# First channel product of the last two groups as seven products of quarters, interleaved with the second

## The chip, the cores and the metric

One core of a Trainium2 chip. The metric is the device time of one execution in microseconds; lower is better. Engines: PE (matmul), DVE, ACT and POOL (elementwise), SP (issues DMAs).

## The reference

Eight batches of linear attention (8 heads, 576 tokens, 64 wide), then an MLP mixer over tokens and over channels. What the change touches is the last step, the channel MLP, on `u` of shape (8, 576, 512):

```
u  = x + (relu(x^T @ w_tok1) @ w_tok2)^T        # 576 -> 256 -> 576 along the tokens
h2 = relu(u @ w_ch1) @ w_ch2                    # 512 -> 1536 -> 512 along the channels
out = u + h2
```

Inputs and output are f32; the kernel multiplies in bf16 and accumulates in f32.

## The kernel before, in words

**Groups.** A batch has 576 tokens: four tiles of 128 and a half tile. `group(g)` for g = 0 to 7 is the four full tiles of batch g (512 tokens); group 8 (`B`) holds the half tiles of all eight batches, again 512 rows. Each group goes through two products: the first, `mlp1` (L315), turns the transposed rows `uT` (channels on the partitions) and `wc1` (512 x 1536) into `h1T` (1536 channels x 512 rows): 12 chunks of 128 channels, each four matmuls of 512 columns, evicted with a relu by ACT (one of the twelve by DVE, L331 and L333). The second is already done by seven products in place of eight: `mlp2_unit` (L372) multiplies quarters of `h1T` and of `wc2`, or sums of quarters, into four PSUM banks called A, X, F and E. A unit is a half of one of the seven products: 6 matmuls of 256 columns (L386); fourteen units make the product. `s_sums` (L356) makes the sums of `h1T` quarters (S1 to S4, bf16) on DVE, `mlp2_sums` (L397) makes the four quarters of the result out of the banks: one copy by ACT (L407), adds out of PSUM by DVE (L409 to L438), and adds of the residual `u` by POOL (L404, six of 128x256 for each group). The results lie in `res`; `store` (L448) writes them out by two DMAs on POOL's queue for each half, `store_tails` (L458) those of group 8 on SP and ACT.

**Order.** The program is scheduled by hand (`manual_schedule`): each engine runs its instructions in the order in which the code issues them, and waits come from the data. For groups 1 to 8 a loop (L1008) runs 26 slots: 12 chunks of the first product in the order `order`, then 14 units of the second. `plan_of(g)` (L933) hangs the other work of the batch pipeline (loads, features, attention, token MLP, transposes) on the slots. Groups 7 and 8 have no such work left but `s_sums`: batch 7, the last, is finished in the slots of group 6 (token MLP at slots 8 to 13, `uT` transposes by DMA from slots 15 and 16, L272; the half tile at slot 18, L298, L303, L306, L307).

**PSUM.** Two tiles `psA` of two banks, four `psM` of one bank; `nextM` and `nextA` hand them out in turn.

**Buffers.** The inputs of the batches are loaded into `raw["q"]`, `raw["k"]`, `raw["v"]` (two buffers each), features in `kp`, `qp`, their transposes in `qpT`. Once the last batch has passed, these are free.

Of the kernel before, what the change touches and what calls it, by code (L numbers as in the profile page):

```python
# [9 lines left out]
F32 = mybir.dt.float32  # L10
BF16 = mybir.dt.bfloat16
I32 = mybir.dt.int32
AF = mybir.ActivationFunctionType
# [5 lines left out]
def kernel(  # L19
# [11 lines left out]
    nc = tc.nc  # L31

    B, H, S, D = q.shape
    F = 2 * D
    Dm = H * D
    D_tok = moe_w_tok1.shape[1]
    D_ch = moe_w_ch1.shape[1]
    P = 128
    assert S == 9 * (P // 2) and D == 64 and H == 8 and B % 2 == 0
    NCC = Dm // P  # L40
    NT = D_tok // P
    NCH = D_ch // P
# [22 lines left out]
    wc1 = sb("w_ch1", [P, NCC, D_ch], BF16)  # L65
    wc2 = sb("w_ch2", [P, NCH, Dm], BF16)

    raw = {n: [sb(f"{n}_raw{i}", [P, H, NJ, D], F32) for i in range(2)] for n in "qkv"}
    kp = [sb(f"kp{j}", [P, H, 2, D], BF16) for j in range(NJ)]
    qp = [sb(f"qp{j}", [P, H, 2, D], BF16) for j in range(NJ)]  # L70
    vb = [sb(f"vb{j}", [P, H, VP], BF16) for j in range(NJ)]

    qpT = sb("qpT", [P, H, NJ, P], BF16)
    at_T = (0, 1, 3, 4, 2)
    kv_sb = sb("kv_sb", [P, H, VP], BF16)
    x_sb = sb("x_sb", [P, T, Dm], BF16)
# [4 lines left out]
    u_sb = [sb(f"u_sb{i}", [P, T, Dm], F32) for i in range(2)]  # L81
# [5 lines left out]
    h1T = sb("h1T", [P, NCH, 4 * P], BF16)  # L87
# [14 lines left out]
    def rows_of(t, i):  # L102
        b = t.rearrange("p h n d -> p h (n d)").bitcast(BF16)
        return b[:, 0:NQ, i * DQ:(i + 1) * DQ]
# [4 lines left out]
    T3, T4 = B12, k1_of[2]  # L109
    S_of = {1: (rows_of(raw["k"][0], 0), rows_of(raw["k"][0], 1), k1_of[0], S4_sb)}  # L110
    for g in range(2, B + 1):
        S_of[g] = (k1_of[0], k1_of[1], rows_of(raw["v"][1], 0), S4_sb)

    LO, HI = slice(0, P // 2), slice(P // 2, P)
    psM, psA = [], []
# [2 lines left out]
    def nextM():  # L118
        cnt["M"] += 1
        return psM[(cnt["M"] - 1) % 4]  # L120

    def nextA():
        cnt["A"] += 1
        return psA[cnt["A"] % 2]
# [185 lines left out]
    def group(g):  # L310
        if g < B:
            return uT[g % 2], u_sb[g % 2]
        return uTt, u_tl
# [42 lines left out]
    def s_sums(g, c0, c1):  # L356
        V = nc.vector
        s1, s2, s3, s4 = [x[:, c0:c1, :] for x in S_of[g]]
        a11, a21 = h1T[:, c0:c1, 0:2 * P], h1T[:, c0:c1, 2 * P:4 * P]
        a12, a22 = h1T[:, NQ + c0:NQ + c1, 0:2 * P], h1T[:, NQ + c0:NQ + c1, 2 * P:4 * P]  # L360
        V.tensor_add(s1, a21, a22)  # L361
        V.tensor_sub(s2, s1, a11)
        if g > 1:
            V.tensor_sub(s3, a11, a21)
        V.tensor_sub(s4, a12, s2)
# [6 lines left out]
    def mlp2_unit(g, i):  # L372

        pr, tt = divmod(i, 2)
        S1, S2, S3, S4 = S_of[g]
        a, w, bank = ((h1T[:, 0:NQ, 0:2 * P], B11, "A"), (S2, T2, "X"), (S3, T3, "F"), (S1, T1, "E"),
                      (h1T[:, NQ:NCH, 0:2 * P], B21, "A"), (h1T[:, NQ:NCH, 2 * P:4 * P], T4, "F"),
                      (S4, B22, "E"))[pr]
        if pr < 4 and tt == 0:
            mbank[bank] = [nextM()[:, 0:2 * DQ].rearrange("p (t d) -> p t d", t=2)] * 2  # L380
            if bank == "E" and g == B:
                mbank["E"][1] = nextA()[:, 0, :].rearrange("p (t d) -> p t d", t=2)
        m = mbank[bank]
        own = m[0] is not m[1]
        for c in range(NQ):
            nc.tensor.matmul(m[tt][:, tt, :], a[:, c, tt * P:(tt + 1) * P], w[:, c, :],  # L386
                             start=(pr < 4 and c == 0 and (tt == 0 or own)),
                             stop=(c == NQ - 1 and (tt == 1 or own) and (pr > 3 or bank == "X")),
                             skip_group_check=True)

    def quarter(g, i, k):

        cols = slice(k * DQ, (k + 1) * DQ)
        return res_all[:, i, :, cols], group(g)[1][:, 2 * i:2 * i + 2, cols]

    def mlp2_sums(g, i):
        V, G = nc.vector, nc.gpsimd  # L397
# [45 lines left out]
    def flush():  # L443
        while stores:
            stores.pop(0)()

    def store(g, t, r):
        if g < B:  # L448
            if t % 2 == 1:
                o = out[g].rearrange("(i n) d -> i n d", n=9)  # L450
                j = t - 1
                nc.gpsimd.dma_start(out=o[:, j:j + 2, :], in_=r[0:P:2, :, :])
                nc.gpsimd.dma_start(out=o[:, 5 + j:5 + j + 2, :], in_=r[1:P:2, :, :])


    tails = out.rearrange("(t b) (i n) d -> (b i) t n d", b=2, n=9)[:, :, 4, :]

    def store_tails(t0, t1, k, eng):  # L458
        cols = slice(k * DQ, (k + 1) * DQ)
        eng.dma_start(out=tails[:, t0:t1, cols], in_=res[t0 // 2][:, t0 % 2:t0 % 2 + t1 - t0, cols])  # L460

# [303 lines left out]
    for mi in (2, 3):  # L767
        mlp1_out(mi, bank_h[mi], (A, V)[mi - 2])
    head.__exit__(None, None, None)
    psum = ctx.enter_context(tc.tile_pool(name="psum", bufs=1, space=bass.MemoryType.PSUM, reuse_waits="tile"))  # L770
    psA += [psum.tile([P, 2, 512], F32, name=f"psA{i}") for i in range(2)]
    psM += [psum.tile([P, 512], F32, name=f"psM{i}") for i in range(4)]

# [159 lines left out]
    def plan_of(g):  # L933
        b, f = g + 1, g + 2
        plan = [[] for _ in range(26)]

        def put(s, fn, *args):
            plan[s].append(lambda: fn(*args))

        if g == 1:  # L940
            put(5, tail_step, 1)
            for j in range(NJ):
                put(j // 2 + 1, f1k, b, j, 0, V)
                put((j + 1) // 2 + 2, kv_step, b, j)
                put(5 + j, num_step, b, j)
            put(3, u_out, 1, 1)
            for i, at in enumerate((4, 4, 17)):
                put(at, t_sum, (1, 3, 2)[i])
            for j in range(NJ):
                put((5, 6, 7, 8, 9)[j], f1k, f, j, 1, A)  # L950
            for j in range(2):
                put(10, f1k, f, j, 0, A)
            put(10, b1_step, b, 0)
            for j in range(2, 4):
                put(11, f1k, f, j, 0, A)
            put(11, b1_step, b, 1)
            put(11, f1k, f, 4, 0, A)
            for n in range(2):
                put(13 + n, u_step, b, n)
                put(15 + n, uturn_step, b, n)  # L960
            put(10, s_sums, g, 0, 3)
            put(11, s_sums, g, 3, 5)
            put(12, s3_sum, g)
            for j in range(3):
                put((12, 13, 15)[j], qfeat, f, j, A, A)
                put((12, 13, 17)[j], qturn_dma, f, j)
            put(17, lambda: feat(A, qp[3][:, :, 1, :], rawt("q", f)[:, :, 3, :], sin_t, 3))
            for j in range(NJ):
                put((18, 18, 19, 20, 21)[j], vcast, f, j, (A, A, V, A, A)[j])
                if j == 2:  # L970
                    put(19, lambda: feat(V, qp[3][:, :, 0, :], rawt("q", f)[:, :, 3, :], cos_t, 3))
                    put(19, qturn_dma, f, 3)
                if j == 3:
                    put(20, qfeat, f, 4, V, A)
                    put(20, qturn_dma, f, 4)
            for j in range(NJ):
                put((23, 24, 25, 25, 25)[j], kv_step, f, j)
            put(8, q_load, 4)
            put(9, v_load, 4)
            put(20, k_load, 4)  # L980
            return plan
        if b < B:
            for j in range(NJ):
                put(((2, 3, 4, 6, 7) if g == 2 else (2, 3, 4, 5, 6))[j], num_step, b, j)
            for n in range(2):
                put(8 + n, b1_step, b, n)
                put(12 + n, u_step, b, n)
                put(15 + n, uturn_step, b, n)
            put(18, tail_step, b)
        if g == 2:  # L990
            put(14, tail_turn, 1)
        for at, cs in ((7, (0, 2)), (9, (2, 4)), (11, (4, 5))):
            put(at, s_sums, g, *cs)
        if f < B:
            for j in range(NJ):
                put((7, 8, 10, 12, 13)[j], qfeat, f, j, V, A)
                put((7, 8, 10, 17, 17)[j], qturn_dma, f, j)
                put((12, 13, 14, 15, 17)[j], f1k, f, j, 0, V)
                put(13 + j, f1k, f, j, 1, A)
                put(j, vcast, f, j, G)  # L1000
                put((20, 21, 22, 24, 25)[j], kv_step, f, j)
        if f + 1 < B:
            put(0, q_load, f + 1)
            put(6, v_load, f + 1)
            put(18, k_load, f + 1)
        return plan

    for g in range(1, B + 1):  # L1008
        plan = plan_of(g)
        for s in range(len(plan)):  # L1010
            if s < NCH:
                ps = mlp1(g, order[s])
            else:
                mlp2_unit(g, s - NCH)
                mlp2_sums(g, s - NCH)
            for fn in plan[s]:
                fn()
            flush()
            if s < NCH:
                mlp1_out(order[s], ps, V if s == 10 else A)  # L1020
                if s == NCH - 1:
                    s_sums(g, NQ - 1, NQ)

    flush()
    _ = tile, bass_utils
# [30 lines left out]
```

## Time and profile before

| what | value |
|---|---|
| median of 12 runs | 262.42 us (260.57 to 264.37) |
| the profiled execution | 264.17 us |
| its span, first to last instruction | 262.4 us |
| PE busy | 250.6 us, 96% of the span |
| DVE / ACT / POOL busy | 189.7 (72%) / 155.4 (59%) / 100.9 (38%) us |
| granted PE clock, mean | 0.992 |
| first product of group 7, of group 8 | 219.45 to 229.81, 238.97 to 249.34 us |
| second product of group 7, of group 8 | 229.81 to 238.97, 249.34 to 258.52 us |

Times inside the span are counted from the first instruction. A row of the profile gives line, engine, operation, what it writes <- what it reads, the shape, the count, and then busy time and mean duration, idle time of the engine before it and who ended it. The chain of waits follows the work that ended last backwards. "PEclk" is the granted clock of PE as a share of the full one.

### The profile page before, as it was taken

The numbers are of one execution on the slowest core, as the hardware profiler recorded it, in microseconds if no ns is written. First come the engines' busy times: TensorE is split into PE (matmuls) and PEld (weight loads), VectorE is DVE, ScalarE is ACT, GpSimd is POOL, SyncE is SP. The second block draws the span as 40 slices with busy tenths as digits, with TensorE's granted clock in tenths as the row PEclk, the third lists the DMA queues.
The fourth block names the chain that finished last, engine by engine and source line by source line (L and its number), as shares of the span: only waits on it lengthen the run. The fifth ranks groups of instructions, "written<-read, shape, count | busy, mean of one in ns | idle before, by whom it ended". The sixth has DMA issues, their size and how long they took to land.

```text
span 262.4 us, 5679 instructions
## 1 busy us (share of the span) xinstructions
PE 250.6 (96%) x2098; PEld 158.2 (60%) x2110; DVE 189.7 (72%) x452; ACT 155.4 (59%) x259; POOL 100.9 (38%) x176
## 2 busy tenths in 40 slices
PE   7799999999999699999999999999999999999994
PEld 2565456455578255775587557755875576486483
DVE  5892857899989079958994899489938773563563
ACT  4763685886998267946783679367935452613610
POOL 5197457270008801194019502830291045045041
PEclk9999999999999799999999999999999999999999
DMA  6999999999999999999978996994391034003004
GB/s 207 366 374 389 390 389 380 303 259 243 262 356 219 257 217 359 210 214 318 350 154 161 373 307 145 173 307 93 68 212 71 4 80 158 24 0 146 17 0 161
DMA packets 79947, 57.18 MB, mean 218 GB/s; under 512 B 48176, under 2 KB 74928, under 8 KB 79920
## 3 DMA queue, kind: packets, MB, share of 16 engines
q1 hardware_dynamic: 76128, 47.26, 68.4%
q0 software_dynamic: 2560, 8.39, 9.4%
q10 hardware_dynamic: 1232, 1.18, 1.4%
q8 instruction: 16, 0.26, 0.4%
q14 instruction: 11, 0.09, 0.1%
HBM read 35.85 MB, written 9.44 MB: 173 GB/s over the span
## 4 chain that ended last, share of the span: by engine, by line
PE 70%; ACT 3%; DVE 1%; DMA 1%; issue 1%; ACTq 0%
PE psM L319 31%; PE psM L386 24%; PE psA L239 5%; PE psA L257 3%; PE psA L214 3%; PE psA L190 2%; DMA uT<-u_bf 1%; PE psA L298 1%; ACT qp L145 1%; ACT u_bf L267 1%; ACT vb L161 1%; PE psA L386 1%; DVE u_sb L262 0%; DVE k_raw L368 0%; ACT kp L145 0%
## 5 line engine op out<-in xcount | busy, mean ns | idle before, releaser
L319 PE MATMUL psM<-uT,w_ch 128*128 128x512 bf16 x368 | 89.7, 384 | 2.4 <-DMA uT<-u_bf 2.4
L331 ACT ACTIVATE h1T<-psM 128x512 bf16<-128x512 f32 x93 | 55.5, 597 | 43.2 <-PE psM L319 41.5
L404 POOL TENSOR_TENSOR res<-res,u_sb 128x256 f32<-128x256 f32 x42 | 32.2, 798 | 96.2 <-DVE res L409 95.8
L319 PEld LDWEIGHTS <-w_ch 128*128 128x128 bf16 x416 | 38.4, 98 | 43.5 <-DMA uT<-u_bf 2.5
L386 PEld LDWEIGHTS <-h1T 128*128 128x128 bf16 x288 | 27.3, 98 | 5.8
L145 ACT ACTIVATE kp<-k_raw,sin_t 128x512 bf16<-128x512 f32 (+1 forms) x45 | 28.4, 669 | 1.2 <-DMA k_raw<-in_k_dram 1.2
L145 ACT ACTIVATE qp<-q_raw,sin_t 128x512 bf16<-128x512 f32 (+1 forms) x40 | 26.6, 681 | 0.1
L386 PE MATMUL psM<-w_ch,h1T 128*128 128x256 bf16 x192 | 25.0, 273 | 0.0
L163 POOL CAST vb<-v_raw 128x512 bf16<-128x512 f32 (+1 forms) x38 | 20.5, 585 | 11.4 <-DMA v_raw<-in_v_dram 10.6
L386 PE MATMUL psM<-w_ch_t,k_raw 128*128 128x256 bf16 x186 | 23.6, 273 | 0.0
L386 PEld LDWEIGHTS <-k_raw 128*128 128x128 bf16 x204 | 19.7, 98 | 5.0 <-issue 1.2
L214 PEld LDWEIGHTS <-qpT 128*128 128x128 bf16 x320 | 14.9, 98 | 9.7 <-issue 1.6
L230 DVE TENSOR_TENSOR x_sb<-psA,rden 128x512 bf16<-128x512 f32 x28 | 19.4, 691 | 1.0
L361 DVE TENSOR_TENSOR k_raw<-h1T 128x512 bf16<-128x512 bf16 (+2 forms) x31 | 11.1, 359 | 12.3 <-ACT h1T L331 11.5
L262 DVE TENSOR_TENSOR u_sb<-psA,x_sb 128x1024 f32<-128x1024 f32 x16 | 19.3, 1214 | 0.1
L226 DVE TENSOR_SCALAR rden<-psA 128x8 f32<-128x8 f32 x35 | 5.7, 163 | 18.4 <-PE psA L214 18.0
L147 DVE TENSOR_SCALAR kp<-k_raw,cos_t 128x512 bf16<-128x512 f32 (+1 forms) x40 | 17.2, 458 | 1.8 <-DMA k_raw<-in_k_dram 1.8
L147 DVE TENSOR_SCALAR qp<-q_raw,cos_t 128x512 bf16<-128x512 f32 (+1 forms) x37 | 16.2, 469 | 2.1 <-DMA q_raw<-in_q_dram 2.1
L257 PE MATMUL psA<-B,w_tok 128*128 128x512 bf16 x64 | 16.4, 379 | 0.0
L214 PE MATMUL psA<-kv_sb,qpT 128*128 128x65 bf16 x280 | 14.3, 193 | 0.3 <-DVE qpT L163 0.3
L239 PE MATMUL psA<-x_sb,w_tok 128*128 128x512 bf16 x49 | 14.0, 379 | 0.6 <-DVE x_sb L230 0.2
L200 ACT CAST kv_sb<-psA 128x520 bf16<-128x520 f32 x7 | 4.2, 604 | 16.7 <-PE psA L190 16.7
(139 smaller groups left out, 392.1 us busy)
## 6 DMA issues: line engine op xcount, KB each, us to landing
out_dram<-res POOLq DMA_DIRECT2D x32, 256.0 KB, 4.8
k_raw<-in_k_dram SPq DMA_DIRECT2D x7, 640.0 KB, 7.4
v_raw<-in_v_dram SPq DMA_DIRECT2D x7, 640.0 KB, 10.4
q_raw<-in_q_dram SPq DMA_DIRECT2D x7, 640.0 KB, 11.1
k_raw<-in_k_dram SPq DMA_DIRECT2D x7, 512.0 KB, 6.3
v_raw<-in_v_dram SPq DMA_DIRECT2D x7, 512.0 KB, 10.2
q_raw<-in_q_dram SPq DMA_DIRECT2D x7, 512.0 KB, 10.2
u_sb<-in_moe_w_ch_dram SPq DMA_DIRECT2D x2, 1024.0 KB, 10.5
```

The source lines that it names most:

```text
L145: eng.activation(out_ap, in_ap, AF.Relu, bias=0.0, scale=s)
L147: eng.tensor_scalar(out_ap, in_ap, scalar1=s, scalar2=0.0, op0=ALU.mult, op1=ALU.max)
L163: eng.tensor_copy(out_ap, in_ap)
L214: nc.tensor.matmul(dst, w, kv_sb[:, h, 0:E1], start=True, stop=True, skip_group_check=True)
L230: nc.vector.tensor_mul(dst.rearrange("p (g h d) -> p g h d", g=2, h=HH), n[:, :, :, 0:D], rb)
L239: nc.tensor.matmul(b1_ps[b][mi], w1[:, jw, mi * P:(mi + 1) * P], x, start=(j == 0), stop=(j == T))
L257: nc.tensor.matmul(ps[:, half, :], w2[:, ki, 2 * c + half, :], B1[b % 2][:, ki, :], start=(ki == 0), stop=(ki == NT - 1))
L262: nc.vector.tensor_add(u_sb[b % 2][:, 2 * c:2 * c + 2, :], ps, x_sb[:, 2 * c:2 * c + 2, :])
L319: nc.tensor.matmul(ps.rearrange("p (t k) -> p t k", k=P), wc1[:, ki, mi * P:(mi + 1) * P], src[:, :, ki, :], start=(ki == 0), stop=(ki == ...
L331: eng.activation(h1T[:, mi, :], ps, AF.Relu)
L386: nc.tensor.matmul(m[tt][:, tt, :], a[:, c, tt * P:(tt + 1) * P], w[:, c, :], start=(pr < 4 and c == 0 and (tt == 0 or own)), stop=(c == N ...
L404: G.tensor_add(c[:, t, :], s[:, t, :], u[:, t, :])
```

## The change

Groups 0 to 6 stay as they are, but for what is hung on the slots of group 6. For groups 7 (`y`) and 8 (`z`) the loop is replaced by a written list in which the units of four products are mixed: the first and second of group 7, the first and second of group 8.

The first product is cut in quarters as the second one is: the channels of `uT` and the rows in halves, `wc1` in halves both ways. Seven products of quarters, W11, W12, W21, W22 or their differences W1 to W4 with the quarters of `u` or their sums, give the four quarters of `h1`. The 768 output channels of a half are worked in three blocks `p` of 256 channels, so there are 21 units (`mlp1_unit(g, p, pr)`), each four matmuls of 256 columns into one bank of PSUM.

- `w_sum`: four differences of `wc1` quarters, 128x1536 bf16, in group 6: two on POOL (slots 0 and 3), two on DVE (slots 17 and 19).
- `u_sums`: four sums of `u` quarters, 128x512 bf16, for group 7 on DVE (slot 24 of group 6), for group 8 on POOL (after the first three units of group 7).
- evictions in `mlp1_unit`, 128x512 f32 each, into twelve buffers `fl` that lie in `kp`, `qp` and `x_sb`: products 1 and 5 copied by ACT, 5 followed by an add on POOL; 6, 7, 4 and 3 added out of PSUM by DVE; 2 with a relu by ACT. Products 2, 4 and 3 accumulate in the banks of 1, 7 and 5.
- `relu_of`: the three other quarters of a block, from `fl` (f32) to `h1` (bf16), by ACT, three of group 7's by DVE.
- `h1_sums`: what `s_sums` did, per block of 512 elements and in three parts; parts of group 8 on POOL.
- group 8's `h1`, its sums and its results lie in freed buffers (`q1`, `v0`, `qpT`, `k0`, `u_sb[0]`), so that it can start while group 7's are read.
- PSUM is cut into eight one-bank tiles for this part.
- the stores of groups 6 and 7 go by SP's queue, not POOL's.

The core of the diff:

```diff
+    W11, W12 = wc1[:, 0:KQ, 0:DH], wc1[:, 0:KQ, DH:D_ch]
+    W21, W22 = wc1[:, KQ:NCC, 0:DH], wc1[:, KQ:NCC, DH:D_ch]
...
+    fl = [t.rearrange("p h a d -> p (h a d)").bitcast(F32) for t in kp + qp]
+    fl += [x_sb[:, 2 * i:2 * i + 2, :].rearrange("p t d -> p (t d)").bitcast(F32) for i in range(2)]
...
+    def w_sum(i, eng):
+        eng.tensor_sub(*((W1, W12, W11), (W2, W22, W1), (W3, W22, W12), (W4, W21, W2))[i - 1])
+    def u_sums(g, V):
...
+        V.tensor_add(s1, a21, a22)
+        V.tensor_sub(s2, s1, a11)
+        V.tensor_sub(s3, a11, a21)
+        V.tensor_sub(s4, a12, s2)
...
+    def mlp1_unit(g, p, pr):
...
+        a, w, n = {1: (src[:, 0:2, 0:KQ, :], W11, "A"), 6: (S2, W2, "X"), 7: (S3, W3, "F"), 5: (S1, W1, "E"),
+                   2: (src[:, 0:2, KQ:NCC, :], W21, "A"), 4: (src[:, 2:4, KQ:NCC, :], W4, "F"),
+                   3: (S4, W22, "E")}[pr]
+        m = banks[g, p, n]
+        first = pr in (1, 6, 7, 5)
+        for mm in range(2):
+            for c in range(KQ):
+                nc.tensor.matmul(m[:, mm, :].rearrange("p (t k) -> p t k", k=P),
+                                 w[:, c, (2 * p + mm) * P:(2 * p + mm + 1) * P], a[:, :, c, :],
...
+        if pr == 1:
+            A.copy(f0, m)
+        elif pr == 6:
+            V.tensor_add(f1, m, f0)
+        elif pr == 7:
+            V.tensor_add(f2, m, f1)
+        elif pr == 5:
+            A.copy(f3, m)
+            G.tensor_add(f3, f3, f2)
+        elif pr == 2:
+            A.activation(c11, m, AF.Relu)
+        elif pr == 4:
+            V.tensor_add(f0, m, f1)
+        else:
+            V.tensor_add(f1, m, f1)
...
+    def h1_sums(g, p, part, V=nc.vector):
...
+        if part == 0:
+            V.tensor_add(s1, a21, a22)
+            V.tensor_sub(s2, s1, a11)
+        elif part == 1:
+            V.tensor_sub(s3, a11, a21)
+        else:
+            V.tensor_sub(s4, a12, s2)
...
+                eng = nc.gpsimd if g < B - 2 else nc.sync
...
+            for at, i, eng in ((0, 3, G), (3, 1, G), (17, 2, V), (19, 4, V)):
+                put(at, w_sum, i, eng)
+            put(24, u_sums, B - 1, V)
...
-    for g in range(1, B + 1):
+    for g in range(1, B - 1):
...
+    for p, bs in enumerate(((h[0], h[3], bA, bE), (h[1], bX, bF, bX), (h[2], h[3], h[0], bA))):
+        for n, bank in zip("AXFE", bs):
+            banks[y, p, n] = bank
+        for n, bank in zip("AXFE", (bF, h[0], bX, bA)):
+            banks[z, p, n] = bank
...
+    run(my(0, 1), my(1, 1), my(2, 1))
+    u_sums(z, G)
+    run(my(0, 6), my(1, 6), my(0, 7), my(1, 7), my(0, 5), my(2, 6), my(0, 2), my(1, 5), my(0, 4),
+        my(1, 2), my(2, 7), my(0, 3), my(1, 4), my(2, 2), my(2, 5), ("r", y, 0, 1), ("r", y, 0, 2),
+        ("r", y, 0, 0), my(1, 3), my(2, 4), ("r", y, 1, 1), ("r", y, 1, 2), my(2, 3), ("r", y, 1, 0, V),
+        ("r", y, 2, 0, V), ("r", y, 2, 1, V), ("r", y, 2, 2), ("s", y, 0, 0), ("s", y, 1, 0), ("s", y, 2, 0))
+    run(("p", y, 0), ("p", y, 1), mz(0, 1), *[("s", y, p, 1) for p in range(3)], mz(0, 6), mz(0, 7), mz(0, 5),
+        ("q", y, 8), ("q", y, 9), mz(0, 2), *[("s", y, p, 2) for p in range(3)],
+        ("p", y, 2), ("p", y, 3), ("p", y, 4), mz(0, 4), mz(0, 3), mz(1, 1),
+        ("r", z, 0, 1), ("r", z, 0, 2), ("r", z, 0, 0),
+        ("p", y, 5), mz(1, 6), mz(1, 7), ("s", z, 0, 0), ("p", y, 6), mz(1, 5), mz(1, 2), ("s", z, 0, 1, G),
+        ("p", y, 7), ("t", y, 9), mz(1, 4), mz(1, 3), mz(2, 1), mz(2, 6), ("p", y, 10),
+        ("r", z, 1, 1), ("r", z, 1, 2), ("r", z, 1, 0), mz(2, 7), ("s", z, 0, 2, G), ("p", y, 11), mz(2, 5),
+        mz(2, 2), mz(2, 4), ("s", z, 1, 0), ("s", z, 1, 1, G), ("r", z, 2, 1), ("r", z, 2, 0), mz(2, 3), ("r", z, 2, 2),
+        ("p", z, 0), ("p", z, 1), ("s", z, 2, 0), ("p", y, 12), ("p", y, 13), ("s", z, 2, 1),
+        ("s", z, 1, 2), ("s", z, 2, 2))
+    run(*[("p", z, i) for i in range(2, 14)])
```

In the list "m" (through `my`, `mz`) is a unit of the first product with its eviction, "r" a relu, "s" a part of `h1_sums`, "p" a unit of the second product with its result sums, "q" a unit without sums, "t" sums without a unit. Group 7's "s" parts 0, 1 and 2 make S1 and S2, S3, and S4.

## The prediction

> **What bounds the kernel now.** I read the chain that ended last first, then the busy table over the four stages that the change touches, then the forms of instructions in these stages, then the timeline where DVE and POOL meet. The last pieces of the chain, in order of time (start, length, what), are:
>
> ```profile
> 219.45 10.36 PE psM L319 x48
> 229.81 9.17 PE psM L386 x84
> 238.97 10.36 PE psM L319 x48
> 249.34 4.58 PE psM L386 x42
> ...
> 258.54 0.42 DVE res L435
> ```
>
> From 219.45 us to the last DVE add nothing but PE is on the chain: group 7's first channel product (48 matmuls of 512 columns, 216 ns each), its second (84 of 256 columns, 109 ns each), and the same for group 8. PE ends at 258.52 us; adds and stores take the rest of the 262.4. The table of the same stages says how full the others are:
>
> ```profile
> core 0: us, PE busy (x) PEld busy (x) DVE busy (x) ACT busy (x) POOL busy (x), PEclk, DMA share, GB/s
> 219.45:229.81 10.36, 10.36 (x50) 4.74 (x49) 4.46 (x11) 5.97 (x10) 2.15 (x4) 1.00 0.26 103
> 229.81:238.97 9.16, 9.16 (x85) 8.16 (x84) 5.31 (x13) 1.18 (x2) 4.15 (x7) 1.00 0.00 0
> 238.97:249.34 10.37, 10.37 (x51) 4.76 (x49) 4.46 (x11) 5.97 (x10) 2.16 (x4) 1.00 0.26 103
> 249.34:258.52 9.18, 9.17 (x84) 7.97 (x82) 5.85 (x15) 1.18 (x2) 4.14 (x6) 1.00 0.10 34
> ```
>
> PE is busy all of the time at full clock (the 1.00); DVE is busy about half (4.5 to 5.9 us of 9 to 10). What one elementwise instruction costs (count | sum, mean ns | idle before):
>
> ```profile
> L409 DVE TENSOR_TENSOR res<-psM,res 128x512 f32<-128x512 f32 x3 | 2.1, 691 | 1.7 <-ACT res L407 1.6
> L361 DVE TENSOR_TENSOR k_raw<-h1T 128x512 bf16<-128x512 bf16 x6 | 2.5, 421 | 10.7 <-ACT h1T L331 10.7
> L404 POOL TENSOR_TENSOR res<-res,u_tl 128x256 f32<-128x256 f32 x6 | 4.1, 716 | 11.7 <-DVE res L409 11.7
> ```
>
> In the timeline a DVE instruction starts before the one ahead has ended: 0.61 us from start to start for an add out of PSUM, 0.34 us for one between SBUF tiles, 0.45 us where it reads the result of the one ahead.
>
> **The gain.** 48 x 216 ns = 10.36 us becomes 84 matmuls of 256 columns (7 products x 3 blocks x 2 x 2) at L386's 109.2 ns = 9.17 us. Twice: 2.38 us. The weight loads (98 ns) stay beside them, as they do beside L386 now. If nothing waits, PE ends at 256.14 us.
>
> **What is added, and where.** Each group's twelve evictions (0.60 us, mostly ACT) become, per block: on DVE four adds out of PSUM, on ACT three evictions and up to three relus, on POOL one 512-wide f32 add; then the four sums for the second product, per block instead of 0.42 and 0.28 us pieces. ACT: some 40 instructions of about 0.5 us in 37 us, not full. The w_sums: two on POOL from 196.2 us, where POOL idles until 213 but for the two x_tc copies, which then come at 203, 11 us before L303 reads them; two on DVE at 0.95 us (L352's form), behind L413 and L419, pushing L303 by 0.4 us and nothing on PE; u_sums of group 7 (4 x 0.42) between L428 and L438, ending at 220.3 us, before the first add is due at 221.3. All of it costs nothing, the cover being DVE's idle there and PE's first three units (1.3 us), which need no sums. The stores moved from POOL to SP free POOL for 2.2 us and are queued behind nothing but older stores; the next write into their tile (group 7's copy, near 231 us) comes some ten us later. The tail from PE's end to the last store stays 3.9 us.
>
> **DVE's queue is where it is decided.** I walked the four engines' written orders with these durations. During group 7's first product DVE keeps up: its twelve adds end at 229.67 us with PE at 228.62. From there DVE never idles until it hands PE the S2 sum of group 8's last block, on which the last twelve units, p(8,2) to p(8,13), 7.9 us of PE, hang (p(g,i) is a half of a second product, as in mlp2_unit). In order:
> - 3 relus x 0.40 (L147's form) = 1.20; group 7's S1, S2: 3 x 0.79 = 2.38; its S3: 3 x 0.34 = 1.02; its S4: 1.02: 5.62.
> - Group 8's adds out of PSUM before that point: 12, less what dependence adds: three pairs X, F at 1.34, six at 0.61: 7.68.
> - Group 7's five result adds in between (L409 to L428): 5 x 0.61 = 3.05.
> - Group 8's S1, S2 of two blocks, 1.58, and the last block's, 0.87: 2.45.
>
> Sum 18.80: ready at 248.47, with two small waits for PE 248.66 us. PE comes there at 219.45 + 42 units x 0.437 + 16 units x 0.655 = 248.28. So without any disturbance PE waits 0.47 us, and ends at **256.6**: 1.9 us gained. There is no slack: each further us on DVE before that point is a us of the whole.
>
> **What disturbs it.** A POOL instruction and a DVE one between SBUF tiles hold each other up (start, length):
>
> ```profile
> 202.50 0.41 DVE L361 TENSOR_TENSOR k_raw<-h1T 128x512 bf16<-128x512 bf16 x1
> 202.65 0.74 POOL L290 COPY x_tc<-x_tl 64x512 bf16<-64x512 bf16 x1 [5.83 <-DVE x_tl L230]
> 202.95 0.72 DVE L362 TENSOR_TENSOR k_raw<-k_raw,h1T 128x512 bf16<-128x512 bf16 x1
> ```
>
> L362 takes 0.42 elsewhere; here it stood 0.30 us until about 0.14 us before POOL was done. The other way round, the same copy took 1.21 us at 49.46 us behind a 0.95 us DVE add. Adds out of PSUM (L413 at 162.60, beside POOL's adds) keep their 0.68. So only the SBUF sums pay, and they are what the change multiplies, while POOL gets 512-wide adds.
>
> Such a POOL add isn't in the trace. Between: not less than the 256-wide one, 0.72 us; not more than two of these, 1.43. The casts give 0.40 us for 256 and 0.61 for 512, so some 0.19 us are fixed; 0.19 + 2 x (0.716 - 0.19) = **1.24** us, which I take, held against DVE for 1.02. For bf16 sums on POOL I take the same (the bf16 copy's 0.62 stands beside the f32 cast's 0.61).
>
> The Trainium skill, "GPSIMD Engine Reference", section 3.1, has 4497 ns for a two-input f32 add of 2048 elements; by a quarter of that, an estimate of 1.12 us, the sum below would end at 259.4 and the time at 263.3.
>
> In the walk four DVE sums meet POOL: S4 of group 7's second block behind the f3 add of block 0 (1.02 us, POOL having asked first), S2 of block 0 behind the f3 add of block 1 (0.91), S1 of block 1 behind the f3 add of block 2 (0.36), S2 of block 1 behind POOL's S3 sum (0.91): 3.20 us. The pairs S1, S2 invite it: DVE lets go for 0.11 us between them, and POOL steps in. PE then waits mainly in three places, for the group-8 evictions at 239.1 and 245.2 (0.9 and 1.1 us) and for S2 at 252.0 (1.4 us), and ends at 256.6 + 3.2 and a restart of 0.1 = **259.89**, which is 1.37 us later than now. From the profiled execution (264.17 us, span 262.4, 1.8 us around it) that makes 265.5; from the median of the runs shown, 262.42 + 1.37 = **263.8**.
>
> **The rivals.**
> - *DVE is not held up at the critical places* (POOL gets its turns while DVE adds out of PSUM, or lets go between its own): PE ends at 256.6, time 262.42 - 1.9 = **260.5**. For it: only about 3 us in 20 are at stake, and a sum that slips past POOL's start escapes; against: L362's 0.72.
> - *POOL's adds are cheap* (0.72 us): the four waits shrink to 1.67 us, PE ends at 258.14: **262.0**.
> - *POOL's adds are dear* (1.43): 4.59 us of waits, PE ends at 261.07: **265.0**.
> - *A PE wait halves the clock.* Where PE stood longest now, it went on slowly (number in brackets: idle before):
>
> ```profile
> 87.61 1.86 PE L319 MATMUL psM<-uT,w_ch 128*128 128x512 bf16 x4 [2.37 <-DMA uT<-u_bf]
> ```
>
> and the stage table has there, with the clock in the third number from the end:
>
> ```profile
> 88.00:92.00 4.00, 4.00 (x17) 1.57 (x16) 0.00 (x0) 1.19 (x2) 3.17 (x6) 0.63 1.06 245
> ```
>
> The twelve matmuls from 87.61 took 4.41 us, elsewhere 2.59: 1.8 us. It decides from a wait near 2.4 us; the walk's longest is 1.4, so the wait before p(8,2) would have to grow by 1 us: 263.8 + 1.0 + 1.8 = **266.6**.
>
> The Trainium skill, "TensorE: Matmul & The Clock Gate", Part 1, lets the clock fall only after an idle window of about 3.4 us; by that none of the waits above would cost clock, though this trace shows it after 2.37.
>
> **How the numbers follow.** About 0.5% (1.3 us) is what a measurement can tell from no change. Forecast (263.8, within 0.7 us of it): 0.45, of which I put 0.20 below 263.73 (within 0.5%) and 0.25 above. Not held up, 260.5: 0.30. Cheap POOL adds, 262.0: 0.05. Dear adds, 265.0: 0.14; clock, 266.6: 0.06. So faster 0.30, same 0.25, slower 0.45. The range takes the fast rival's 260.5 less 0.3 and goes up past the dear adds to 266.0, leaving out the clock case and the ends, under 2 in 10. Of the forecast alone: 263.1 to 264.5.
>
> **What would show it.** After: 168 matmuls of 109 ns in the two first products; PE without waits until about 235.8; DVE busy without a break from 229 to the S2 sum; DVE sums of 0.7 to 1.4 us instead of 0.42 where POOL runs; a POOL add of 128x512 near 1.24 us; PE waits on DVE near 239, 245 and 252. Wrong if those sums stay at 0.42, if PE waits early (POOL's sums of the tail group late), or if DVE has idle time there.

## The result, and the profile after

The changed kernel takes **264.99 us** (median of 12 runs, 264.17 to 266.31; a thirteenth on record took 262.78) against 262.37 us for the kernel before (49 runs): a ratio of 1.0098, 95% interval 1.0073 to 1.0123, so it is slower by 2.6 us. The forecast was 263.8 us, with a range from 260.2 to 266.0.

The profiled execution of the changed kernel took 264.35 us, with a span of 262.6. It reached group 7's first product at 217.15 us, the one of before at 219.45; in the other kernels below, whose work up to there is nearly the same, this start lies between 216.2 and 219.3 us. So the length of the stage is compared (first matmul of group 7's first product to the last matmul), not the clock time: **39.07 us before, 41.95 us after**, 2.9 us more.

Profile after, the chain that ended last (start, length, what), its pieces about the two places that matter:

```profile
217.15 2.20 PE psY L442 x20
...
219.45 1.37 DVE k_raw L426
220.82 0.61 DVE res L537
...
234.94 2.16 DVE h_s L485 x3
...
241.48 1.37 DVE qpT L481
...
251.50 7.61 PE psY L410 x68
259.14 0.42 DVE u_sb L534
```

Before, nothing but PE stood here. Now DVE's sums (L426, L485, L481) are on the chain, and only the last 68 matmuls are PE's alone again. By stretches of the stage, PE busy, PEld, DVE, ACT, POOL, granted clock:

```profile
217.15:226.00 8.85, 7.75 (x70) 6.41 (x68) 8.85 (x12) 3.82 (x7) 7.11 (x6) 1.00 0.30 120
226.00:235.00 9.00, 8.85 (x80) 7.61 (x78) 8.36 (x20) 6.24 (x12) 1.28 (x1) 1.00 0.00 0
235.00:247.00 12.00, 10.11 (x87) 8.47 (x87) 11.49 (x19) 6.05 (x11) 9.19 (x10) 1.00 0.01 1
247.00:259.10 12.10, 11.61 (x104) 9.91 (x103) 9.80 (x18) 2.88 (x6) 6.71 (x8) 1.00 0.30 116
```

DVE, half idle before, is busy 8.85 of 8.85 us in the first stretch and 11.49 of 12.00 in the third, and in these two, where POOL is busiest (7.11 and 9.19 us), PE has its largest holes, 1.1 and 1.9 us. (A sum that is held up counts as busy, so these shares hold the hold-ups too; e3 below tells them apart. PE's busy time hides a part of each wait: a matmul's record is 0.27 us long where the next one starts 0.11 us after it. So the length of the stage, not the sum of the holes, says what was lost.) The clock column stays at 1.00: no wait cost clock. In what PE waited for, all of it is DVE (us in total, times, longest):

```profile
PE psY L442 <- DVE kp L461: 1.7, 2, 1.0
PE psY L442 <- DVE res L537: 0.8, 1, 0.8
PE psY L410 <- DVE qpT L481: 0.5, 1, 0.5
PE psY L442 <- DVE k_raw L425: 0.3, 1, 0.3
PE psY L442 <- DVE kp L454: 0.2, 1, 0.2
```

L461 is the eviction of product 4 of group 8, L481 its S2, L454 the eviction of product 7: late in the stage, as forecast. L425 is `u_sums` of group 7, and L537 is group 6's result add that stands right behind these sums in DVE's queue: at the very start of the stage, as not forecast. The timeline there:

```profile
216.49 0.41 DVE L423 TENSOR_TENSOR k_raw<-uT 128x512 bf16<-128x512 bf16 x1
...
216.79 1.16 POOL L423 TENSOR_TENSOR v_raw<-uTt 128x512 bf16<-128x512 bf16 x1 [0.33 <-DMA uTt<-u_bt]
216.93 1.29 DVE L424 TENSOR_TENSOR k_raw<-k_raw,uT 128x512 bf16<-128x512 bf16 x1
...
218.03 1.22 POOL L424 TENSOR_TENSOR v_raw<-v_raw,uTt 128x512 bf16<-128x512 bf16 x1
218.15 1.37 DVE L425 TENSOR_TENSOR k_raw<-uT 128x512 bf16<-128x512 bf16 x1
...
219.20 1.33 POOL L425 TENSOR_TENSOR v_raw<-uTt 128x512 bf16<-128x512 bf16 x1
219.45 1.37 DVE L426 TENSOR_TENSOR k_raw<-uT,k_raw 128x512 bf16<-128x512 bf16 x1
```

DVE's first sum takes 0.41 us. Then POOL starts the same sums for group 8, and the three other sums of DVE take 1.29 to 1.37 us, each ending 0.27 to 0.29 us after the POOL sum ahead of it: DVE's 1.29 from 216.93 ends at 218.22, POOL's 1.16 from 216.79 at 217.95. Of its own 0.42 us, then, a sum has some two thirds still to do when POOL's record ends, so it was held until about 0.14 us before that. The same in the later places, where the prediction had looked for it:

```profile
232.54 1.09 DVE L483 TENSOR_TENSOR v_raw<-h1T 128x512 bf16<-128x512 bf16 x3
...
234.94 2.16 DVE L485 TENSOR_TENSOR h_s<-h1T,k_raw 128x512 bf16<-128x512 bf16 x3
...
235.17 1.31 POOL L457 TENSOR_TENSOR kp<-kp,kp 128x512 f32<-128x512 f32 x1 [6.48 <-DVE kp L454]
...
241.26 1.31 POOL L457 TENSOR_TENSOR qp<-qp,qp 128x512 f32<-128x512 f32 x1 [0.69 <-DVE qp L454]
241.48 1.37 DVE L481 TENSOR_TENSOR qpT<-qpT,q_raw 128x512 bf16<-128x512 bf16 x1
...
248.43 1.34 POOL L483 TENSOR_TENSOR qpT<-q_raw 128x512 bf16<-128x512 bf16 x1
248.79 1.26 DVE L481 TENSOR_TENSOR qpT<-qpT,q_raw 128x512 bf16<-128x512 bf16 x1
```

Three sums in a row take 1.09 us undisturbed (L483 at 232.54); at 234.94, beside POOL's f3 add (L457, behind product 5), 2.16.

### The profile page after: what moved, and what is told of

Read it like the earlier page. It is cut to its first block, busy times and chain, and to the rows that moved or that the text cites. A ratio compares the mean times of both kernels' runs of the same rounds, so it can differ in the third digit from the quotient of the medians.

```text
span 262.6 us, 5879 instructions
## 1 busy us (share of the span) xinstructions
PE 249.3 (95%) x2170; PEld 165.4 (63%) x2182; DVE 211.8 (81%) x472; ACT 160.0 (61%) x270; POOL 120.7 (46%) x183
## 4 chain that ended last, share of the span: by engine, by line
PE 62%; DVE 8%; DMA 3%; issue 2%; DVEq 0%
PE psM L410 21%; PE psM L345 20%; PE psA L265 5%; PE psA L283 4%; PE psY L442 3%; DMA qpT<-qp 3%; PE psY L410 3%; PE psA L216 3%; PE psA L240 3%; PE psA L324 1%; DVE h_s L485 1%; DVE qpT L481 1%; DVE qp L463 1%; DVE qp L461 1%; DVE k_raw L426 1%
## 5 line engine op out<-in xcount | busy, mean ns | idle before, releaser
L345 PE MATMUL psM<-uT,w_ch 128*128 128x512 bf16 x320 | 77.5, 379 | 0.0
L503 POOL TENSOR_TENSOR res<-res,u_sb 128x256 f32<-128x256 f32 x42 | 33.7, 835 | 85.1 <-DVE res L508 75.6
L357 ACT ACTIVATE h1T<-psM 128x512 bf16<-128x512 f32 x71 | 42.3, 596 | 19.6 <-PE psM L345 19.0
L345 PEld LDWEIGHTS <-w_ch 128*128 128x128 bf16 x320 | 28.6, 97 | 28.9 <-issue 0.2
L410 PEld LDWEIGHTS <-h1T 128*128 128x128 bf16 x252 | 23.8, 98 | 5.1
L410 PEld LDWEIGHTS <-k_raw 128*128 128x128 bf16 x192 | 18.6, 98 | 4.8 <-issue 1.2
L173 DVE TENSOR_SCALAR kp<-k_raw,cos_t 128x512 bf16<-128x512 f32 (+1 forms) x40 | 18.1, 482 | 1.7 <-DMA k_raw<-in_k_dram 1.7
L410 PE MATMUL psM<-w_ch,h1T 128*128 128x256 bf16 x144 | 19.1, 273 | 0.0
L410 PE MATMUL psM<-w_ch_t,k_raw 128*128 128x256 bf16 x144 | 18.4, 273 | 0.0
L271 ACT ACTIVATE B<-psA 128x512 bf16<-128x512 f32 x13 | 7.8, 597 | 10.1 <-PE psA L265 10.0
```

Source lines behind the costliest of these rows:

```text
L173: eng.tensor_scalar(out_ap, in_ap, scalar1=s, scalar2=0.0, op0=ALU.mult, op1=ALU.max)
L345: nc.tensor.matmul(ps.rearrange("p (t k) -> p t k", k=P), wc1[:, ki, mi * P:(mi + 1) * P], src[:, :, ki, :], start=(ki == 0), stop=(ki == ...
L357: eng.activation(h1T[:, mi, :], ps, AF.Relu)
L503: G.tensor_add(c[:, t, :], s[:, t, :], u[:, t, :])
```

## The experiments

The theory: POOL's 512-wide sums hold up DVE's sums between SBUF tiles; with no slack in DVE's queue this is what PE waits for. Rivals: DVE's queue is too long by itself, whatever POOL does; POOL disturbs by being busy and not by what it reads; the work added to group 6 costs something; mixing the units is a bad order as such. The table gives the length of the stage in each profiled execution (from the chain), and the measured time against the kernel before. The ratios are those on record, against executions of the kernel before from the same series (medians 262.37, 262.18 for e1 to e4, 262.16 for e5 to e8); they are not the quotients of the medians, from which e3's is furthest (0.9925 against 0.997).

| kernel | stage, us | median, us | ratio (95% interval) |
|---|---|---|---|
| before | 39.07 | 262.37 | 1 |
| after | 41.95 | 264.99 | 1.0098 (1.0073 to 1.0123) |
| e1: u_sums of group 7 earlier | 41.86 | 264.43 | 1.0079 (1.0048 to 1.0109) |
| e2: POOL's sums 64 wide | 37.81 | 260.68 | 0.9942 (0.9915 to 0.9968) |
| e3: POOL writes, reads nothing | 37.69 | 261.34 | 0.9925 (0.9888 to 0.9961) |
| e4: only the work in group 6 | 39.07 | 261.81 | 0.9992 (0.9967 to 1.0018) |
| e5: other order, three f3 adds on DVE | 36.79 | 259.91 | 0.9912 (0.9882 to 0.9941) |
| e6: u_sums of group 8 on DVE | 40.63 | 263.33 | 1.0056 (1.0030 to 1.0082) |
| e7: not interleaved | 44.50 | 268.35 | 1.0229 (1.0189 to 1.0269) |
| e8: before, with added POOL adds | 53.12 | 277.55 | 1.0549 (1.0504 to 1.0594) |

**e1, the sums of group 7 earlier.**

```diff
-            put(24, u_sums, B - 1, V)
+            put(20, u_sums, B - 1, V)
```

> Group 7's four sums of u quarters on DVE at slot 20 of group 6 in place of slot 24, nothing else. Theory (hold-ups between DVE and POOL sums): they end before POOL starts group 8's sums, so the first PE waits (1.4 us up to the eighth unit) go; PE waits fall from 5.3 to about 3.9 us, the time from 265.0 to about 263.6 (ratio to before 1.004). Rival (DVE simply has too much to do from 219 to 251, whatever POOL does): the same work is done earlier, the queue behind it is as long, and the time stays within 0.4 us of 265.0.

Four slots earlier changed almost nothing: the stage is 0.1 us shorter. The timeline says why:

```profile
215.41 0.97 DVE L416 TENSOR_TENSOR k_raw<-w_ch,q_raw 128x1536 bf16<-128x1536 bf16 x1
216.30 0.94 DVE L423 TENSOR_TENSOR k_raw<-uT 128x512 bf16<-128x512 bf16 x1
217.27 0.83 DVE L424 TENSOR_TENSOR k_raw<-k_raw,uT 128x512 bf16<-128x512 bf16 x1
217.99 1.15 POOL L423 TENSOR_TENSOR v_raw<-uTt 128x512 bf16<-128x512 bf16 x1 [0.17 <-DMA uTt<-u_bt]
218.03 1.40 DVE L425 TENSOR_TENSOR k_raw<-uT 128x512 bf16<-128x512 bf16 x1
219.35 1.37 DVE L426 TENSOR_TENSOR k_raw<-uT,k_raw 128x512 bf16<-128x512 bf16 x1
```

DVE works in order and came to them only behind the weight difference W4 (L416), 2.05 us ahead of the stage's start in place of 0.66. The first two then met POOL's residual adds of group 6 (212.06 to 217.8 us), the last two met POOL's `u_sums`. The partner changed, the price did not. The edit missed what it was meant to separate; e6 does that.

**e2, POOL's sums narrow.** Each sum that the change gave to POOL handles 64 of 512 columns.

```diff
-            G.tensor_add(f3, f3, f2)
+            G.tensor_add(f3[:, :, 0:32], f3[:, :, 0:32], f2[:, :, 0:32])
```

(and the like in `u_sums` and `h1_sums` where the engine is POOL; the rest of their tiles is filled once in group 6)

> Leaves out 7/8 of POOL's new sums (64 of 512 columns; the rest of these tiles is not the sum), so that each takes some 0.3 us; DVE, ACT and PE do all that they did. Theory (hold-ups): DVE's sums stay near 0.42 us, PE waits fall from 5.3 to at most 0.8 us, time about 260.3 (ratio 0.992). Rival (DVE's own queue is what PE waits for): waits stay at 3.5 us or more, time at least 263.

**e3, POOL writes but does not read.** Each of these POOL sums becomes two memsets of the same tile.

```diff
-            G.tensor_add(f3, f3, f2)
+            G.memset(f3, 0.5)
+            G.memset(f3, 0.5)
```

(and the like in `u_sums` and `h1_sums`)

> Leaves out POOL's new sums: in place of each stand two memsets of the same tile, some 1.0 us together, that read nothing. If it is POOL's reading of SBUF that holds DVE's two-input sums up: these stay near 0.42 us, time near 260.5, though POOL is busy nearly as long. If any POOL instruction holds them up, or if PE waits for POOL's late results: DVE sums of 0.7 to 1.4 us as after, time 264 or more.

Both are faster than before: the stage shrinks from 41.95 to 37.81 and 37.69 us. So DVE's queue by itself is not what costs the time; POOL's sums cost 4.1 to 4.3 us. The whole stage, after and in e3:

```profile
217.15:259.10 41.95, 38.31 (x337) 32.40 (x334) 38.50 (x65) 19.00 (x35) 24.30 (x25) 1.00 0.15 59
217.77:255.46 37.69, 37.33 (x337) 32.57 (x334) 33.02 (x65) 19.07 (x35) 20.89 (x37) 1.00 0.17 66
```

DVE runs the same 65 instructions and is busy 33.02 us in place of 38.50: some 5.5 us of its time were hold-ups. The start of the stage in e3:

```profile
217.01 0.51 POOL L425 MEMSET v_raw<- 128x512 bf16 x1
217.11 0.41 DVE L428 TENSOR_TENSOR k_raw<-uT 128x512 bf16<-128x512 bf16 x1
217.56 0.42 DVE L429 TENSOR_TENSOR k_raw<-k_raw,uT 128x512 bf16<-128x512 bf16 x1
217.59 0.53 POOL L426 MEMSET v_raw<- 128x512 bf16 x1
217.90 0.42 DVE L430 TENSOR_TENSOR k_raw<-uT 128x512 bf16<-128x512 bf16 x1
218.05 0.52 POOL L425 MEMSET v_raw<- 128x512 bf16 x1
```

POOL is as good as busy throughout (two memsets, 1.05 us, where a sum took 1.16 to 1.33), and DVE's sums keep their 0.42. What holds DVE up is that POOL **reads** SBUF, not that it works or writes. The Trainium skill, "SBUF — State Buffer", section "Who interferes with whom", says this: a DVE instruction with two SBUF inputs contends with a GpSimd (POOL) instruction that reads SBUF, not with one that only writes it. These rows agree, 0.42 us beside memsets and 1.29 to 1.37 beside sums.

**e4, only the work in group 6.** The change's weight differences, `u_sums` of group 7 and stores by SP are kept; from group 7 on the loop of before runs, and what was prepared is not used.

```diff
-    for g in range(1, B - 1):
+    for g in range(1, B + 1):
```

> Groups 7 and 8 as before (48 matmuls of 512 columns each); kept of the change: the differences of w_ch1 quarters, group 7's u sums (both unused) and the stores of groups 6 and 7 on SP's queue. Theory: all of it is hidden in group 6, time 262.4 (ratio 0.998 to 1.002). Rival (they push something of group 6 that is on the path): 263 or more.

The time is that of before and the stage is 39.07 us again: the additions ahead of the stage are free. All of the loss arises inside it.

**e6, the early meeting taken away.** `u_sums` of group 8 goes to DVE, where it stood on POOL; nothing else moves.

```diff
-    u_sums(z, G)
+    u_sums(z, V)
```

(in substance: the run's kernel writes the list out, with the same units in the same order)

> Group 8's four sums of u quarters on DVE, behind group 7's, in place of POOL; the rest as after. Theory: the early collision (DVE sums of 1.3 to 1.4 us at 217 to 221) goes, the four more sums cost DVE 1.4 us while PE needs it less; PE waits fall by 1.2 to 1.8 us, time 263.2 to 263.8, ratio about 1.004. Rival (DVE's load counts, not the meeting): waits grow by up to 1.4 us, time 266.

The stage is 1.3 us shorter, although DVE got four more sums. The waits that stay are the later ones, of the same size as after:

```profile
PE psY L442 <- DVE kp L464: 1.7, 2, 1.0
PE psY L410 <- DVE qpT L485: 0.5, 1, 0.5
PE psY L442 <- DVE kp L454: 0.2, 1, 0.2
```

Eight undisturbed sums on one engine (0.41 to 0.42 us each) took less of DVE's time than four that meet four on POOL.

**e7, the interleaving taken away.** The same 168 matmuls and the same sums, but group 8's first product only after all of group 7's second.

```diff
-    run(("p", y, 0), ("p", y, 1), mz(0, 1), *[("s", y, p, 1) for p in range(3)], mz(0, 6), mz(0, 7), mz(0, 5),
+    run(("p", y, 0), ("p", y, 1), *[("s", y, p, 1) for p in range(3)],
```

(and so on: the `mz` units follow `("p", y, 13)`)

> The units of the four products are not interleaved: all of group 7's, then all of group 8's, in the order that each has now. Theory: DVE's and ACT's work bunches behind each first product and PE waits for it; some 3.2 us more waiting than after, time about 268. Rival (the order is of no weight, since DVE's total is the same): time within 0.6 us of 265.

The stage grows to 44.50 us. PE's waits become more and longer (1.7 us once for an ACT copy of the results, 1.0, 0.8, 0.5 and 0.5 for DVE). So interleaving is not the fault. The chain there suggests why: without it a block's chain of evictions and sums has no other units to stand behind.

**e8, POOL adds in the kernel before.** Nine adds of 128x512 f32 on POOL, whose results nobody uses, in chunks 6 to 11 of the first products of groups 7 and 8.

```diff
+        if g >= B - 1:
+            fl = [t.rearrange("p h a d -> p (h a d)").bitcast(F32) for t in kp + qp]
+            for i in range(9):
+                put((6, 7, 7, 8, 9, 9, 10, 11, 11)[i], G.tensor_add, fl[i], fl[(i + 1) % 9], fl[9])
```

> The kernel before with nine f32 adds of 128x512 on POOL, of unused data, in the first product of groups 7 and 8. Theory: DVE's sums there are held up (0.42 us to 0.7 or more, some of them to 1.4), but DVE is busy half of the time, so little of it reaches PE: time 262.2 to 262.9, ratio below 1.003. Rival (a held-up sum goes straight to the time): the ratio 1.008 or more.

This is the largest miss: 5.5% slower, where I had thought that a DVE with half of its time idle would swallow the hold-ups. The timeline of DVE, POOL and PE:

```profile
218.37 5.44 POOL L938 TENSOR_TENSOR kp<-kp,qp 128x512 f32<-128x512 f32 x4
...
222.61 1.49 DVE L364 TENSOR_TENSOR v_raw<-h1T 128x512 bf16<-128x512 bf16 x1
223.89 1.33 POOL L938 TENSOR_TENSOR kp<-qp,qp 128x512 f32<-128x512 f32 x1
224.02 1.49 DVE L365 TENSOR_TENSOR h_s<-h1T,k_raw 128x512 bf16<-128x512 bf16 x1
...
232.50 0.28 PE L386 MATMUL psM<-w_ch_t,k_raw 128*128 128x256 bf16 x1 [3.74 <-DVE k_raw L362]
```

POOL runs without a gap, and DVE gets one sum in between two of POOL's: each of its eight 512-wide sums takes 0.90 to 1.49 us instead of 0.42, about 1 us more. Eight of these come to some 8 us within about 11, more than the 5.9 us that DVE idled in the same product before, and the last S2, on which PE's second product hangs, is late by 3.74 us at once. The same comes again in group 8: PE waits 9.2 us in all, in six pieces, for S2. After these waits PE also runs slowly (stretch, length, PE, PEld, DVE, ACT, POOL, clock):

```profile
229.88:233.29 3.41, 0.28 (x1) 0.10 (x1) 3.24 (x8) 0.00 (x0) 0.96 (x1) 1.00 0.00 0
233.29:236.70 3.41, 3.27 (x16) 2.34 (x17) 1.18 (x4) 0.00 (x0) 0.73 (x2) 0.50 0.00 0
236.80:241.00 4.20, 4.20 (x41) 3.77 (x39) 2.07 (x3) 0.00 (x0) 3.36 (x5) 1.00 0.00 0
...
253.75:257.16 3.41, 1.03 (x8) 0.43 (x6) 3.41 (x3) 0.59 (x1) 3.25 (x3) 1.00 0.00 0
```

The clock is 0.50 for 3.41 us, and 1.00 again behind it; in group 8 it falls at 257.16, 2.1 us into a wait of 3.74, and stays at 0.50 until 264.0. So the mechanism holds without the change too, and the clock of the prediction's rival does fall where PE idles enough: it did here, and with the waits of at most 1.0 us after it did not.

The length of the wait alone does not decide it. The four turns of the clock (233.29, 236.70, 257.16, 264.0) lie whole multiples of 3.41 us apart, and each fall stands behind a stretch of 3.41 us in which PE was busy for 0.28 or 1.03 us; in the trace of before it was 1.08 us (84.16 to 87.57), and the clock was then 0.50 until 91.0. A stretch with 2.02 us (226.47 to 229.88) cost nothing. That the share of such a stretch decides is inferred from these three falls. The Trainium skill, "TensorE: Matmul & The Clock Gate", Part 1, puts the fall after an idle window of about 3.4 us. The length of the window agrees with the steps here; that it has to be idle throughout does not, since PE was busy for 1.03 and 1.08 us of it.

**e5, the work kept, the order changed.** Another written order of the same units: `u_sums` of group 8 later, S1 and S2 apart, the relus of group 7 all on ACT, other parts of group 8's sums on POOL. For three of the six blocks, f3 is one DVE add out of PSUM in place of ACT's copy and POOL's add.

```diff
-            A.copy(f3, m)
-            G.tensor_add(f3, f3, f2)
+            if (B - g, p) in ((1, 2), (0, 1), (0, 2)):
+                V.tensor_add(f3, m, f2)
+            else:
+                A.copy(f3, m)
+                G.tensor_add(f3, f3, f2)
...
-    run(my(0, 1), my(1, 1), my(2, 1))
-    u_sums(z, G)
+    run(
+        ("m", y, 0, 1), ("m", y, 0, 6), ("m", y, 1, 1), ("m", y, 0, 7), ("m", y, 0, 5), ("m", y, 1, 6),
+        ("m", y, 1, 7), ("m", y, 2, 1), ("m", y, 0, 2), ("m", y, 0, 4), ("m", y, 1, 4), ("m", y, 0, 3),
+        ("m", y, 2, 6), ("r", y, 0, 0), ("m", y, 2, 7), ("r", y, 1, 1), ("u", z, G), ("m", y, 1, 2),
...
```

> Computes all that the changed kernel computes; the written order of groups 7 and 8 is another one (found by walking the queues with the durations and the hold-up that the runs showed), three of the six f3 quarters are made by one DVE add out of PSUM in place of an ACT copy and a POOL add, the three relus on DVE become one or none, and POOL's sums stand where DVE adds out of PSUM. Theory (the seven products are worth their 2.4 us where DVE's SBUF sums and POOL's do not meet ahead of a unit that PE needs): PE waits of the stage at most 0.8 us in place of 5.3, time 260.0 to 260.9, ratio 0.991 to 0.995. Rival (DVE has too much to do in any order): waits of 2.5 us or more, time 262.5 or more.

259.91 us, 0.9912 (0.9882 to 0.9941): this version beats both kernels. The stage in one row, as above:

```profile
219.28:256.07 36.79, 36.77 (x336) 32.53 (x334) 33.67 (x65) 18.96 (x35) 20.79 (x22) 1.00 0.17 68
```

PE is busy 36.77 of 36.79 us: the whole gain of 2.3 us is there (39.07 - 36.79), with POOL still busy for 20.8 us and DVE for 33.7. The forms of its sums:

```profile
L485 DVE TENSOR_TENSOR k_raw<-k_raw,h1T 128x512 bf16<-128x512 bf16 x3 | 1.2, 415 | 0.0
L483 DVE TENSOR_TENSOR k_raw<-h1T 128x512 bf16<-128x512 bf16 x3 | 1.2, 414 | 0.0
L485 DVE TENSOR_TENSOR qpT<-qpT,q_raw 128x512 bf16<-128x512 bf16 x2 | 1.4, 678 | 0.0
```

Nearly all are at 0.41 to 0.42 us; the third row shows what is left. POOL's `u_sums` (1.15 to 1.16 us each, from 223.53) now run while DVE adds out of PSUM, and those adds stay at 0.68 to 0.69 us. Which of this version's edits carries how much was not separated.

## Why the prediction was right, and where it was not

The forecast of a small loss held in sign and mechanism, and the measured 2.6 us lie within the range; the size was 1.2 us too small, and 264.99 us lies outside the 263.1 to 264.5 that were given for the forecast alone. Its terms, for PE's waits in the stage:

| term | predicted, us | measured, us | from |
|---|---|---|---|
| PE's work without waits | 36.7 (39.07 - 2.38) | 36.79 | e5 |
| waits if POOL holds nothing up | 0.47 | 0.9 | e3 37.69, less 36.79 |
| POOL's sums, later places | 3.20 and 0.1 | 2.9 | e6 40.63, less e3 |
| POOL's sums, at the start | 0 | 1.3 | after 41.95, less e6 |

**The step that failed** is "All of it costs nothing": `u_sums` of group 7 were priced at 4 x 0.42 us, done 1.0 us before DVE's first add is due. They took 4.3 us, since POOL's four sums for group 8 stood beside them; the prediction had looked for such meetings only from group 7's S4 on. It named the sign of it ("if PE waits early"), but gave it no price. In my walk the transpose `uTt` came 3.4 us after its issue (the median of the four in the trace of before), so POOL would have started behind DVE; in the trace it is issued at 214.36 and POOL starts on it at 216.79, 2.4 us later. That the order of arrival decides is argued from these two numbers; that the meeting costs 1.3 us is shown by e6. The sums ended 3.7 us into the stage (220.82), where the prediction had 0.9 (220.3): some 2.8 us late, and the 1.0 us of slack and PE's first units hid about half of it.

**The steps that held.**
- The gain: 168 matmuls at 109 ns. In e5, where nothing waits, the stage is 2.28 us shorter, against 2.38.
- DVE without slack: 11.49 of 12.00 us in the third stretch, hold-ups included (without them, in e3, 33.02 of the stage's 37.69). The waits without hold-ups were set too low (0.47 against 0.9): in e3 PE still waits for evictions of group 8.
- POOL's 512-wide f32 add: 1.24 us estimated, 1.28 to 1.30 measured, the bf16 sums 1.16 to 1.34.
- The hold-ups: S4 of block 1 was put at 1.02 and cost 1.07 (2.16 - 1.09), S2 of block 0 at 0.91 and cost 0.95 (1.37 - 0.42), S1 and S2 of block 1 at 0.36 and 0.91 and cost 0.18 and 0.84: 3.04 against 3.20.
- PE's later waits: forecast near 239.1, 245.2 and 252.0 us. Less 2.3 for the earlier start of the stage and plus 1.4 for the waits at its start (by 222.07 PE had done 32 matmuls, 3.5 us of work, in 4.9), that is 238.2, 244.3 and 251.1; they came at 238.35, 244.70 and 251.50, with 0.71, 0.97 and 0.49 us against 0.9, 1.1 and 1.4. The last came out smaller, presumably since PE had already been kept back elsewhere.
- The tail of 3.9 us became 3.5 (259.10 to 262.6).

**Sums that do not close.** The wait without hold-ups is 0.38 us by the prediction's own figures (248.66 less 248.28), where it says 0.47; and 256.6 with 1.67 or 4.59 added is 258.3 or 261.2, where the rivals of cheap and dear adds have 258.14 and 261.07. None of this moves a time by more than 0.2 us. The 0.40 us of the 256-wide cast, behind the estimate of 1.24 for POOL's add, is the least of eight; their mean is 0.45.

**The rivals.** "Not held up", priced 260.5, is what e2 does: 260.68. "Cheap adds" fell with the 1.28 us. "Dear adds", 265.0, has the right time for the wrong reason: POOL's adds took 1.28 to 1.30 us, not 1.43. The clock stayed at 1.00 in the change; e8 shows that it falls where PE idles enough.

## What to carry to other kernels

A change that trades PE work for elementwise sums must be counted on DVE and POOL as one resource wherever a DVE sum reads two SBUF tiles while POOL reads SBUF, from the first sum on and not only where the queue is full. Put POOL's sums beside DVE's adds out of PSUM, and keep DVE's sums between SBUF tiles for POOL's pauses: e5 does this, and with the same products, and three of POOL's adds moved to DVE, it made 264.99 us into 259.91. Idle time of DVE is a cover only if POOL pauses in it (e8).

## What the runs showed of the hardware that was not expected

- A POOL sum that reads SBUF raised a DVE sum beside it from 0.42 to between 0.60 and 1.49 us. POOL's memsets beside it left it at 0.42. Adds out of PSUM stayed at 0.67 to 0.69 us beside POOL's sums.
- Against a POOL that runs without a gap, DVE got one sum for each of POOL's (e8: 1.37 to 1.49 us from L362 on). Two streams of sums side by side so run at POOL's pace, some three times slower than DVE alone.
- In e8, PE ran at a clock of 0.50 from 233.29 to 236.70 us, behind waits of 3.74 and 0.65 us: twelve matmuls took 2.36 us from 234.90 and 1.47 behind it. In group 8 the clock was down already 2.1 us into the wait, for 6.8 us. Waits up to 1.0 us, after, left the clock at 1.00.
